# Moving the gate's row sums from the value projection into the attention stage, and giving the value copies five places instead of two

## The chip, the cores and the metric

The kernel runs on one core of a Trainium2 chip. The metric is the device time of one execution in microseconds (us): 2908.87 us is the median of three runs of the kernel before (2906.5 to 2911.03). The core's engines work side by side, each through its own fixed list of instructions in order: PE (matrix products), DVE (vector engine), ACT (activations and copies), POOL (GpSimd) and SP, which here only issues DMA transfers. They wait for one another through semaphores.

## The reference

Two attention blocks read the same x (2048 rows of 1024) and are mixed by a gate, all in float32:

```python
g = sigmoid((x * gate_w).sum(-1, keepdims=True))   # the gate: one number per row of x
a = linear_attention(x, A_wqkv, A_wo)   # 32 heads of 32; phi(t) = where(t>0, t+1, exp(t)) + 1e-6
b = softmax_attention(x, B_wqkv, B_wo)  # 32 heads of 32, 2048 x 2048 scores each
return g * a + (1 - g) * b
```

The gate needs, for each of the 16 blocks of 128 rows, a product of x with gate_w and a sum over its 1024 columns. It is used first where the queries of the linear attention are divided (g) and at the output (1 - g).

## The kernel before, in words

Every large matrix product is done as three products of "hi" and "lo" parts (lines 146 to 148 in `three`), so one product of a block of 128 rows with 512 columns is 8 x 3 = 24 matmuls, called a unit here.

The program has three parts. First (0 to 401 us) q, k and half of v of the softmax attention are computed; POOL and DVE prepare operands there (lines 253 and 409 to 414). Second (401 to 534 us), the stream `linear()` computes the second half of v in 16 "v" units; between their matmuls the stream `maxima()` puts score matmuls (line 902) whose row maxima DVE takes with a reduce (line 907). Third (from 534 us), the softmax heads run (`heads_()`: score matmuls of line 1053, exponentials on ACT in line 1057, products with v in line 1149), and at the same time maxima of a later head and the units of the linear attention: 64 units of keys and values ("kv"; a chunk is 16 units), 32 of queries, 32 of output. In this stage the sums of the exponentials are split: POOL adds 1536 of 2048 columns with one add per block (lines 1098 and 1102), DVE the other 512 (line 1111), which it keeps in a PSUM bank.

The order is written out by a planner at build time: it keeps a clock `T` per engine, takes the stream that is ready or furthest behind, and lets it issue. PSUM has a ring of six banks for all streams: a matmul can start in a bank only after the reader of that bank's former content has ended. Work on DVE that may come later is handed to `defer(fn, at, cost, rank)` and issued by `fill` where the planner's clock of DVE has room, or by `need` where something depends on it. An engine then goes through its list strictly in order.

The gate before (function `gate`, called by `next(gating, None)` at the end of each v unit): for each block t, two DMA loads of x into a quarter each of big[20] (line 334), and two DVE instructions SCALAR_TENSOR_TENSOR (line 344) that multiply by gate_w (in `zrep`) and sum along the row; both inputs lie in SBUF. One block is loaded ahead. After the sixteenth block follow an add, an Exp on ACT (line 347), and three small DVE instructions.

At the end of a v unit, ACT copies the unit's bank to a tile in SBUF (line 365), which SP sends to DRAM (line 366). The tile alternates between mid[10] and mid[11]. At the end of the last v unit the weights of the next chunk arrive by DMA (line 260), ACT and DVE split them (lines 571 and 573), and the copy of the unit's bank stands behind that on ACT.

Of the kernel before, what the change touches and what calls it, by code (L numbers as in the profile page):

```python
# [11 lines left out]
AF = mybir.ActivationFunctionType  # L12
ALU = mybir.AluOpType
# [5 lines left out]
P = 128  # L19
DH = 32  # L20
C = 512
# [24 lines left out]
def kernel(  # L46
# [107 lines left out]
    def use(eng, cost, *after):  # L154

        T[eng] = max(T[eng], *after, 0.0) + cost
        return T[eng] + LATENCY[eng]
# [142 lines left out]
    PAIRS = [(j, j + 1) for j in range(0, NJ, 2)]  # L300
    tmp = f32(big[20])
    s1, u2, u3 = [tmp[:, i * C:(i + 1) * C] for i in range(3)]
    gate_x = [tmp[:, i * C:(i + 1) * C] for i in range(4)]

    def xop(name, p, i):
        return big[XO[name][p]][:, i * C:(i + 1) * C]
# [20 lines left out]

    HD = D // 2
    nc.sync.dma_start(zrep, bass.AP(tensor=gate_w.tensor, offset=gate_w.offset, ap=[[0, P], [1, D]]))

    def gate():
        def load(t):
            for i in range(2):
                nc.sync.dma_start(gate_x[t % 2 * 2 + i], x[t * P:(t + 1) * P, i * HD:(i + 1) * HD])

        load(0)
        for t in range(NT):
            yield
            if t + 1 < NT:
                load(t + 1)  # L340
            for i in range(2):
                gx = gate_x[t % 2 * 2 + i]
                use("dve", 0.7)
                nc.vector.scalar_tensor_tensor(gx, gx, 1.0, zrep[:, i * HD:(i + 1) * HD], op0=ALU.mult,
                                               op1=ALU.mult, accum_out=tg[:, i, t:t + 1])
        nc.vector.tensor_add(tg[:, 0], tg[:, 0], tg[:, 1])
        nc.scalar.activation(tg[:, 0], tg[:, 0], AF.Exp, scale=-1.0)
        nc.vector.tensor_scalar_add(tg[:, 0], tg[:, 0], 1.0)
        nc.vector.reciprocal(g_sb, tg[:, 0])
        nc.vector.tensor_scalar(omg_sb, g_sb, -1.0, 1.0, op0=ALU.mult, op1=ALU.add)  # L350

    def spill(js):

# [10 lines left out]
    def v_out(c, t, ps, va):  # L364
        nc.scalar.copy(va, ps)
        nc.sync.dma_start(v_d[c][:, t, :], va)
# [75 lines left out]
        nc.sync.dma_start(qk_d[sec][0][g][:, sl], f32(hi))  # L442
        nc.sync.dma_start(qk_d[sec][1][g][:, sl], f32(lo))

    gating = gate()
    xp_done = set()

    def first_xp(n):
# [249 lines left out]
    def queries(n, c, t, pq, todo):  # L698
# [19 lines left out]
        give(b, 0.0, [item])  # L718
        o_left.append(item)

    def linear():
        extra = iter(())
        coming_w = deque()
        for n, (i, t) in enumerate(units):
            kind, c = chunks[i]
            pos = n % NT
            here_ = n < NT // 2
            follow = chunks[i + 1] if i + 1 < len(chunks) else None
            xp = xp_t[n % 2]
            yield bank_at  # L730
            b = take()
            ps = bank[b]
            T["pe"] = max(T["pe"], free[b])
            lin_kind[0] = kind
            if kind in ("q", "o") and c == 0 and t in (2, 8, NT - 2):
                yield lambda: None if mix_here else 0.0
                if t < NT - 2:
                    load_mix()
            if n < 2:
                load_head(n)  # L740
                load_v(n)
            for k in range(NK):
                yield lambda: ended(w_left[k], w_ready[k], 0.0 if here_ else xp_ready[n % 2])
                need(w_left[k])
                if here_:
                    jj, tt = divmod(n, TPC)
                    stat = [xop(PLACE[jj][k // HK], p, k % HK)[:, tt * P:(tt + 1) * P] for p in range(2)]
                else:
                    stat = [blocks(xp, p)[:, k] for p in range(2)]
                for m, _ in enumerate(three(ps, stat, (wpart(k, 0), wpart(k, 1)), k)):  # L750
                    lin_pe(1.0)
                    if m < 2:
                        yield always
                if k == 0 and n + 7 == len(units) and not o_main[0]:
                    load_o(0)
                if k == 1 and n + 1 == len(units):
                    split_o(0, slice(0, NK - 1))
                if k == NK // 2 and n + 1 == len(units) and over["head"]:
                    split_o(1, slice(0, NK - 1))
                if k == NK - 1:  # L760
                    yield from extra
                if follow and follow[0] == "o":
                    if pos == NT - 1:
                        w_left[k].clear()
                        yield lambda: 0.0 if mixed.count((k // HK, follow[1])) == 4 else None
                        load_wa(follow[1], k)
                    continue
                if follow and pos == NT - 2 and k < min(LEAD_W, NK):
                    coming_w.append(load_w(*follow, k, LEAD_W + 1))
                if follow and pos == NT - 1:  # L770
                    split_w(*follow, k, *coming_w.popleft(), nc.vector if kind == "v" else nc.gpsimd)
                    if k + LEAD_W < NK:
                        coming_w.append(load_w(*follow, k + LEAD_W, LEAD_W + 1))
            if NT // 2 <= n + 2 < len(units):
                load_xp(n + 2)
            for _ in range(1 + (n == 1) if n < NT else 0):
                next(gating, None)
            extra = iter(())
            e, r = mid[3 + n % 3], mid[6]
            if kind == "v":  # L780
                give(b, use("act", 0.5, T["pe"] + LATENCY["pe"]))
                v_out(c, t, ps, mid[10 + t % 2])
            elif kind == "kv":
                va = mid[7][:, (n % 2) * HC:(n % 2 + 1) * HC]
                yield from keys_alone(n - 2)
                nc.scalar.copy(va, ps[:, HC:])
                use("act", 0.28, T["pe"] + LATENCY["pe"])
                end = phi(ps, e, HC)

                def more(end, c=c, t=t, e=e, ps=ps):  # L790
                    pk = e[:, :HC]
                    nc.vector.scalar_tensor_tensor(pk, pk, 1.0, ps[:, :HC], op0=ALU.min, op1=ALU.add)
                    z_end[c % 2] = use("pool", 0.69, end)
                    if t == 0:
                        nc.gpsimd.tensor_copy(zsum[c % 2], pk)
                    else:
                        nc.gpsimd.tensor_add(zsum[c % 2], zsum[c % 2], pk)

                todo = [defer(more, end, 0.34)]
                give(b, 0.0, todo)  # L800
                keys(n, c, t, e, va, todo)
                if t == NT - 1:
                    extra = keysum(c)
            elif kind == "q":
                yield lambda: None if n - 3 not in turned and chunks[units[n - 3][0]][0] == "q" else 0.0
                end = phi(ps, e, C)
                d = dn[n % 2]

                def sums(_, e=e, ps=ps):
                    nc.vector.scalar_tensor_tensor(ps, e, 1.0, ps, op0=ALU.min, op1=ALU.add)  # L810

                def scaled(_, c=c, ps=ps, r=r):
                    nc.vector.tensor_mul(r, ps, zrep[:, c * C:(c + 1) * C])

                last = []

                def dens(end, r=r, d=d, last=last):
                    nc.vector.tensor_reduce(d, r.rearrange("p (h d) -> p h d", d=DH), AX.X, ALU.add)
                    nc.scalar.add(d, d, eps)
                    last[0].at = use("act", 0.2, end)  # L820

                def divide(_, t=t, e=e, ps=ps, d=d):
                    nc.vector.reciprocal(d, d)
                    nc.vector.scalar_tensor_tensor(
                        e.rearrange("p (h d) -> p h d", d=DH), ps.rearrange("p (h d) -> p h d", d=DH),
                        g_sb[:, t:t + 1], d.unsqueeze(2).to_broadcast([P, C // DH, DH]),
                        op0=ALU.mult, op1=ALU.mult)

                todo = chain(((sums, 0.63), (scaled, 0.63), (dens, 0.63), (divide, 0.9)), end)
                last.append(todo[-1])  # L830
                give(b, 0.0, todo)
                tasks.append((lambda todo=todo: both(ended(todo + o_left), bank_at()),
                              lambda n=n, c=c, t=t, e=e, todo=todo: queries(n, c, t, e, todo)))
            else:
                res = mid[(7, 10)[n % 2]]
                give(b, use("act", 0.5, T["pe"] + LATENCY["pe"]))
                nc.scalar.copy(res, ps)
                nc.sync.dma_start(ra_d[t][:, c * C:(c + 1) * C], res)
        over["lin"] = True
        load_all()  # L840
# [548 lines left out]
```

## Time and profile before

| | before |
|---|---|
| median of 3 runs | 2908.87 us |
| the profiled execution, its own time | 2906.63 us |
| span of that execution on the core | 2904.8 us |
| busy share: PE, DVE, ACT, POOL | 98%, 77%, 55%, 64% |
| mean DMA rate | 138 GB/s |

The span is the time from the first to the last instruction in the trace; the execution's own time is 1.8 us longer. A busy share is an average over the three parts, and says little of any one of them: POOL, for instance, is idle through the v units and almost always busy in the attention stage.

### The profile page before, as it was taken

To read this page: it belongs to the slowest core of one execution; us is meant where nothing else is said; L and a number is where in the kernel's file an instruction comes from. 1 tells how busy PE (TensorE), PEld (TensorE's weight loads), DVE (VectorE), ACT (ScalarE), POOL (GpSimd) and SP (SyncE) were. 2 spreads that over 40 slices of the span, in tenths; PEclk is the share of its full clock that TensorE was granted. 3 is DMA by queue.
4 is the path that set the end of the run, shared out by engine and by line. 5 is a ranking of instruction groups with operands and counts; after the bars stand their busy time and mean duration, and the time that the engine had idled before them with its cause. 6 is when DMAs were issued, how large, how long until landed. Compare 5 with 4: busy or idle time off the path is not lost.

```text
span 2904.8 us, 44336 instructions
## 1 busy us (share of the span) xinstructions
PE 2847.1 (98%) x15744; PEld 2039.5 (70%) x15744; DVE 2227.9 (77%) x3715; ACT 1596.8 (55%) x2976; POOL 1853.9 (64%) x646
## 2 busy tenths in 40 slices
PE   9999989899999999999999999799999999999999
PEld 7888867666666766666666666467676666766787
DVE  6667638788888888888888888688888887886522
ACT  5334320566676667666666666456666665666410
POOL 1212220488798889987988888468777878785000
PEclk9999999999999999999999999899999999999999
DMA  5957765423332324233323235444455344524542
GB/s 174 291 173 216 243 202 189 156 91 98 99 117 76 93 88 120 89 102 92 117 80 91 88 120 165 157 166 146 146 175 182 112 146 127 153 88 140 171 158 78
DMA packets 302496, 400.55 MB, mean 138 GB/s; under 512 B 92682, under 2 KB 185354, under 8 KB 299146
## 3 DMA queue, kind: packets, MB, share of 16 engines
q1 hardware_dynamic: 302276, 397.73, 44.3%
q8 instruction: 124, 2.03, 0.3%
q14 instruction: 96, 0.79, 0.1%
HBM read 287.57 MB, written 108.79 MB: 136 GB/s over the span
## 4 chain that ended last, share of the span: by engine, by line
PE 94%; DMA 3%; DVE 2%; ACT 0%; issue 0%; SPq 0%; ACTq 0%; DVEq 0%
PE bank L1053 16%; PE bank L902 16%; PE bank L1149 15%; PE bank L146 11%; PE bank L148 10%; PE bank L147 10%; PE bank L430 3%; PE bank L432 3%; PE bank L431 3%; PE bank L472 1%; PE bank L955 1%; PE bank L470 1%; PE bank L471 1%; DMA big<-xs 1%; DMA big<-qk 0%; PE bank L707 0%
## 5 line engine op out<-in xcount | busy, mean ns | idle before, releaser
L1102 POOL TENSOR_TENSOR big<-big,big 128x1536 f32<-128x1536 f32 (+1 forms) x434 | 1556.5, 3586 | 209.0 <-ACT big L1057 186.9
L907 DVE TENSOR_REDUCE mx<-bank 128x1 f32<-128x512 f32 x2048 | 1308.7, 680 | 306.7 <-PE bank L902 301.8
L1057 ACT ACTIVATE big<-bank 128x512 f32<-128x512 f32 x2048 | 1180.1, 601 | 528.1 <-PE bank L1053 457.8
L902 PE MATMUL bank<-big,big 128*128 128x512 f32 x2048 | 804.8, 393 | 21.6 <-DVE mx L907 11.9
L1053 PE MATMUL bank<-big,big 128*128 128x512 f32 x2048 | 810.7, 397 | 2.2 <-ACT big L1057 2.0
L146 PE MATMUL bank<-big,big 128*128 128x512 f32 x1408 | 554.6, 394 | 25.4 <-DMA big<-xs 21.4
L148 PE MATMUL bank<-big,big 128*128 128x512 f32 x1408 | 552.6, 392 | 1.0 <-DMA big<-oA 0.8
L147 PE MATMUL bank<-big,big 128*128 128x512 f32 x1408 | 552.8, 393 | 0.0
L1053 PEld LDWEIGHTS bank<-big,big 128*128 128x128 f32 x2048 | 384.4, 188 | 159.8 <-issue 62.8
L902 PEld LDWEIGHTS bank<-big,big 128*128 128x128 f32 x2048 | 385.9, 188 | 106.4 <-DVE mx L907 12.6
L1149 PE MATMUL bank<-big,mid 128*32 128x512 f32 x4096 | 459.2, 593 | 0.0
L146 PEld LDWEIGHTS bank<-big,big 128*128 128x128 f32 x1408 | 265.8, 189 | 91.2 <-issue 19.2
L1149 PEld LDWEIGHTS bank<-big,mid 128*32 128x32 f32 x4096 | 127.7, 110 | 263.6 <-issue 263.6
L148 PEld LDWEIGHTS bank<-big,big 128*128 128x128 f32 x1408 | 266.0, 189 | 58.5 <-DMA big<-oA 1.2
L147 PEld LDWEIGHTS bank<-big,big 128*128 128x128 f32 x1408 | 265.9, 189 | 55.4
L1111 DVE TENSOR_TENSOR bank<-bank,big 128x512 f32<-128x512 f32 (+1 forms) x434 | 280.2, 646 | 7.6 <-ACT big L1057 5.7
L1098 POOL TENSOR_TENSOR big<-big,big 128x1536 f32<-128x1536 f32 (+1 forms) x31 | 111.6, 3601 | 264.7 <-issue 141.1
L253 DVE TENSOR_TENSOR big<-mid,big 128x512 fp32r<-128x512 f32 x216 | 152.8, 731 | 83.9 <-ACT big L252 83.8
L409 POOL TENSOR_TENSOR mid<-mid,mid 128x512 f32<-128x512 f32 x16 | 20.7, 1291 | 278.3 <-DVE big L253 265.3
L252 ACT CAST big<-mid 128x512 fp32r<-128x512 f32 x216 | 130.2, 624 | 100.9 <-POOL mid L410 55.3
L431 PE MATMUL bank<-big,big 128*128 128x512 f32 x448 | 174.3, 389 | 0.0
L432 PE MATMUL bank<-big,big 128*128 128x512 f32 x448 | 174.3, 389 | 0.0
(102 smaller groups left out, 1949.8 us busy)
## 6 DMA issues: line engine op xcount, KB each, us to landing
big<-xs SPq DMA_DIRECT2D x208, 512.0 KB
qk<-mid SPq DMA_DIRECT2D x128, 256.0 KB
big<-oA SPq DMA_DIRECT2D x64, 512.0 KB
big<-qk SPq DMA_DIRECT2D x96, 256.0 KB
big<-qk SPq DMA_DIRECT2D x384, 64.0 KB
mid<-in_b_wqkv SPq DMA_DIRECT2D x88, 256.0 KB
xs<-big SPq DMA_DIRECT2D x64, 256.0 KB
oA<-mid SPq DMA_DIRECT2D x64, 256.0 KB
```

The source lines that it names most:

```text
L146: yield nc.tensor.matmul(ps, sh, mh_, start=(kt == 0), stop=False)
L147: yield nc.tensor.matmul(ps, sh, ml_, start=False, stop=False)
L148: yield nc.tensor.matmul(ps, sl, mh_, start=False, stop=(kt == NK - 1))
L431: nc.tensor.matmul(ps, sh, ml_, start=False, stop=False)
L432: nc.tensor.matmul(ps, sl, mh_, start=False, stop=(i == HK - 1))
L902: nc.tensor.matmul(bank[b], q[:, t * P:(t + 1) * P], k[:, j * C:(j + 1) * C], start=True, stop=True)
L907: nc.vector.tensor_reduce(m[:, t, j:j + 1], bank[b], AX.X, ALU.max)
L1053: nc.tensor.matmul(bank[b], k[:, t * P:(t + 1) * P], q[:, j * C:(j + 1) * C], start=True, stop=True)
L1057: nc.scalar.activation(pr_t[i][:, j * C:(j + 1) * C], bank[b], AF.Exp, scale=SCALE)
L1102: nc.gpsimd.tensor_add(lacc[:, :qp], lacc[:, :qp], pr(t)[:, :qp])
L1111: nc.vector.tensor_add(lacc[:, qp:] if t == NT - 1 else l_b[:, :n], l_b[:, :n], src)
L1149: nc.tensor.matmul(av_b[j * DH:(j + 1) * DH, :], v[:, t, :], pr(t)[:, j * C:(j + 1) * C], start=(t == 0), stop=(t == NT - 1))
```

## The change: what it does

The generator `gate()` with its early start is gone. A function `gate(t)` is called at the end of the last v unit and of the first sixteen kv units (units 15 to 31). It first issues what is left of the previous block's work (`need`), then loads the two halves of block t into mid[8] and mid[9], and defers the two SCALAR_TENSOR_TENSOR instructions (planned at 8 us after the planner's PE clock, 0.7 us each, rank 2). The last call does the final arithmetic. So the same 32 loads and 32 instructions are issued, in kv units instead of v units. The copies of v's second half go round mid[10], mid[11], mid[7], mid[8], mid[9].

```diff
-    gate_x = [tmp[:, i * C:(i + 1) * C] for i in range(4)]
...
-    def gate():
-        def load(t):
-            for i in range(2):
-                nc.sync.dma_start(gate_x[t % 2 * 2 + i], x[t * P:(t + 1) * P, i * HD:(i + 1) * HD])
-
-        load(0)
-        for t in range(NT):
-            yield
-            if t + 1 < NT:
-                load(t + 1)
-            for i in range(2):
-                gx = gate_x[t % 2 * 2 + i]
-                use("dve", 0.7)
-                nc.vector.scalar_tensor_tensor(gx, gx, 1.0, zrep[:, i * HD:(i + 1) * HD], op0=ALU.mult,
-                                               op1=ALU.mult, accum_out=tg[:, i, t:t + 1])
-        nc.vector.tensor_add(tg[:, 0], tg[:, 0], tg[:, 1])
...
-    gating = gate()
...
+    def gate(t):
+
+        need(gates)
+        gates.clear()
+        at = T["pe"] + 8.0
+        for i in range(2 if t < NT else 0):
+            gx = mid[8 + i]
+            nc.sync.dma_start(gx, x[t * P:(t + 1) * P, i * HD:(i + 1) * HD])
+
+            def part(_, i=i, gx=gx):
+                nc.vector.scalar_tensor_tensor(gx, gx, 1.0, zrep[:, i * HD:(i + 1) * HD], op0=ALU.mult,
+                                               op1=ALU.mult, accum_out=tg[:, i, t:t + 1])
+
+            gates.append(defer(part, at, 0.7, 2))
+        if t == NT:
+            nc.vector.tensor_add(tg[:, 0], tg[:, 0], tg[:, 1])
...
+            use("dve", 0.8)
...
-            for _ in range(1 + (n == 1) if n < NT else 0):
-                next(gating, None)
+            if NT - 1 <= n < 2 * NT:
+                gate(n - NT + 1)
...
-                v_out(c, t, ps, mid[10 + t % 2])
+                v_out(c, t, ps, mid[(10, 11, 7, 8, 9)[n % 5]])
```

On DVE, at the third v unit, where the first maxima stand. Names: `mx` is the tile of maxima, `bank5` a PSUM bank, `big20` the loaded x, `zrep` gate_w, `tg` the gate's sums. Before:

```order
L253 TENSOR_TENSOR big19_227<-mid13_242,big19_227 128x512
L344 SCALAR_TENSOR_TENSOR big20_228,tg_199<-big20_228,zrep_196 128x512 x6
L907 TENSOR_REDUCE mx0_200<-bank5_248 128x1
L907 TENSOR_REDUCE mx0_200<-bank6_249 128x1
L907 TENSOR_REDUCE mx0_200<-bank0_243 128x1
```

After:

```order
L253 TENSOR_TENSOR big19_227<-mid13_242,big19_227 128x512
L908 TENSOR_REDUCE mx0_200<-bank5_248 128x1
L908 TENSOR_REDUCE mx0_200<-bank6_249 128x1
L908 TENSOR_REDUCE mx0_200<-bank0_243 128x1
L908 TENSOR_REDUCE mx0_200<-bank1_244 128x1
```

Six gate instructions stood ahead of the first maximum; now none does, and none stands among the other maxima of the v units.

On DVE, in the attention stage, where a head's sums are inverted (RECIPROCAL) and its result is scaled. Names: `kvb` is the sum of the linear attention's keys times values, `mid11` the head's result, `big9`/`big10` exponentials, `bank7` DVE's part of their sum, `mid8` and `mid9` the loaded x. Before:

```order
L1111 TENSOR_TENSOR bank7_250<-bank7_250,big9_3822 128x512
L907 TENSOR_REDUCE mx0_200<-bank0_243 128x1
L617 TENSOR_TENSOR kvb_195<-bank3_246,kvb_195 128x64
L962 RECIPROCAL bank2_245<-bank2_245 128x128 x4
L965 TENSOR_TENSOR mid11_240<-mid11_240,bank2_245 128x512
L907 TENSOR_REDUCE mx0_200<-bank1_244 128x1
```

After:

```order
L1112 TENSOR_TENSOR bank7_250<-bank7_250,big9_3755 128x512
L908 TENSOR_REDUCE mx0_200<-bank2_245 128x1
L908 TENSOR_REDUCE mx0_200<-bank1_244 128x1
L594 TENSOR_TENSOR kvb_195<-bank0_243,kvb_195 128x64
L708 SCALAR_TENSOR_TENSOR mid8_237,tg_199<-mid8_237,zrep_196 128x512
L708 SCALAR_TENSOR_TENSOR mid9_238,tg_199<-mid9_238,zrep_196 128x512
L963 RECIPROCAL bank6_249<-bank6_249 128x128 x4
L966 TENSOR_TENSOR mid11_240<-mid11_240,bank6_249 128x512
L908 TENSOR_REDUCE mx0_200<-bank1_244 128x1
```

One pair of gate instructions now stands ahead of the reciprocals and of the maxima behind them. There are 16 such pairs in the kv units; ten stand together like this one, the other six have maxima between the two.

On SP, in the v units. Names: `v1` is the second half of v in DRAM, `in_x` the input x, `mid13<-v0` the load of a head's v. Before:

```order
L886 DMA mid13_242<-v0_160 128x16x32
L334 DMA big20_228<-in_x 128x512 x4
L366 DMA v1_161<-mid11_240 128x512
L334 DMA big20_228<-in_x 128x512 x2
L366 DMA v1_161<-mid10_239 128x512
```

After:

```order
L887 DMA mid13_242<-v0_160 128x16x32
L344 DMA v1_161<-mid11_240 128x512
L344 DMA v1_161<-mid7_236 128x512
L344 DMA v1_161<-mid8_237 128x512
L344 DMA v1_161<-mid9_238 128x512
```

The loads of x have left this stretch, and three more tiles take the copies of v. PE's list is the same before and after up to the first kv unit; from there to the end of the sixteenth a few matmuls change places, and behind it the lists agree again.

## Rows read from the trace of the kernel before

**Rows 1.** The page's busy time: busy us, share of the span, instructions.
```profile
PE 2847.1 (98%) x15744; PEld 2039.5 (70%) x15744; DVE 2227.9 (77%) x3715; ACT 1596.8 (55%) x2976; POOL 1853.9 (64%) x646
```

**Rows 2.** Waits of PE, whole span: us in total, times, longest us.
```profile
PE bank L146 <- DMA big<-xs: 21.4, 2, 15.0
PE bank L902 <- DVE mx L907: 11.9, 1, 11.9
PE bank L902 <- ACT mid L365: 9.5, 2, 6.8
```

**Rows 3.** Timeline of PE, third v unit: start, us, instruction [idle before <-releaser].
```profile
421.53 0.39 PE L146 MATMUL bank<-big,big 128*128 128x512 f32 x1
424.56 0.79 PE L902 MATMUL bank<-big,big 128*128 128x512 f32 x1 [2.64 <-ACT mid L365]
...
438.49 0.80 PE L902 MATMUL bank<-big,big 128*128 128x512 f32 x1 [11.86 <-DVE mx L907]
439.08 0.63 PE L147 MATMUL bank<-big,big 128*128 128x512 f32 x1
...
441.58 0.39 PE L146 MATMUL bank<-big,big 128*128 128x512 f32 x1
441.81 0.39 PE L147 MATMUL bank<-big,big 128*128 128x512 f32 x1
```

**Rows 4.** Timeline of ACT, same stretch.
```profile
423.92 0.58 ACT L365 COPY mid<-bank 128x512 f32<-128x512 f32 x1 [11.35 <-DMA v<-mid]
```

**Rows 5.** Timeline of DVE, same stretch.
```profile
434.85 0.69 DVE L344 SCALAR_TENSOR_TENSOR big<-big,zrep 128x512 f32<-128x512 f32 x1 [11.07 <-DMA big<-in_x]
...
437.75 4.40 DVE L907 TENSOR_REDUCE mx<-bank 128x1 f32<-128x512 f32 x7
```

**Rows 6.** Timeline of PE, from the last v unit into the first kv unit.
```profile
522.45 0.39 PE L148 MATMUL bank<-big,big 128*128 128x512 f32 x1
...
526.90 0.40 PE L147 MATMUL bank<-big,big 128*128 128x512 f32 x1
534.15 0.79 PE L902 MATMUL bank<-big,big 128*128 128x512 f32 x1 [6.85 <-ACT mid L365]
...
537.21 0.39 PE L146 MATMUL bank<-big,big 128*128 128x512 f32 x1
```

**Rows 7.** Timeline of ACT, same stretch.
```profile
529.16 2.06 ACT L571 CAST big<-mid 128x512 fp32r<-128x512 f32 x3 [4.93 <-DMA mid<-in_a_wqkv]
533.41 0.22 ACT L347 ACTIVATE tg<-tg 128x16 f32<-128x16 f32 x1 [2.19 <-DVE tg L346]
533.53 0.57 ACT L365 COPY mid<-bank 128x512 f32<-128x512 f32 x1
```

**Rows 8.** Windows: stretch, its length, busy us of each engine, granted clock, DMA share, GB/s.
```profile
510.00:530.00 20.00, 15.17 (x66) 11.92 (x64) 10.75 (x21) 5.01 (x9) 0.00 (x0) 1.00 0.90 303
540.00:850.00 310.00, 310.00 (x1899) 212.01 (x1898) 265.19 (x455) 206.23 (x400) 269.21 (x96) 1.00 0.31 95
```

**Rows 9.** Waits of DVE from 540 to 850 us.
```profile
DVE mx L907 <- PE bank L902: 41.2, 14, 4.5
```

**Rows 10.** POOL's groups from 540 to 850 us: count, busy us, mean ns, idle before.
```profile
L1102 POOL TENSOR_TENSOR big<-big,big 128x1536 f32<-128x1536 f32 x67 | 234.6, 3502 | 20.7 <-ACT big L1057 17.5
```

**Rows 11.** Timeline of DVE in the first part, beside POOL's adds.
```profile
256.80 0.68 DVE L493 TENSOR_TENSOR big<-bank,big 128x512 f32<-128x512 f32 x1
257.40 1.40 DVE L253 TENSOR_TENSOR big<-mid,big 128x512 fp32r<-128x512 f32 x1
260.63 1.11 DVE L253 TENSOR_TENSOR big<-mid,big 128x512 fp32r<-128x512 f32 x1 [1.83 <-ACT big L252]
```

**Rows 12.** Timeline of POOL, same stretch.
```profile
256.96 1.28 POOL L409 TENSOR_TENSOR mid<-mid,mid 128x512 f32<-128x512 f32 x1 [4.65 <-DVE big L253]
258.32 1.62 POOL L410 TENSOR_TENSOR mid<-mid,mid 128x512 f32<-128x512 f32 x1
259.90 1.29 POOL L411 TENSOR_TENSOR mid<-mid,mid 128x512 f32<-128x512 f32 x1
```

More of the change, by code (lines that the diff above doesn't have):

```diff
@@ L329 @@
     nc.sync.dma_start(zrep, bass.AP(tensor=gate_w.tensor, offset=gate_w.offset, ap=[[0, P], [1, D]]))
-    def gate():
-        def load(t):
-            for i in range(2):
-                nc.sync.dma_start(gate_x[t % 2 * 2 + i], x[t * P:(t + 1) * P, i * HD:(i + 1) * HD])
-        load(0)
-        for t in range(NT):
-            yield
-            if t + 1 < NT:
-                load(t + 1)
-            for i in range(2):
-                gx = gate_x[t % 2 * 2 + i]
-                use("dve", 0.7)
-                nc.vector.scalar_tensor_tensor(gx, gx, 1.0, zrep[:, i * HD:(i + 1) * HD], op0=ALU.mult,
-                                               op1=ALU.mult, accum_out=tg[:, i, t:t + 1])
-        nc.vector.tensor_add(tg[:, 0], tg[:, 0], tg[:, 1])
[L347 to L350, printed above, removed]
     def spill(js):
@@ L719, in queries @@
         o_left.append(item)
+    def gate(t):
[11 more added lines that the diff above has]
+            nc.vector.tensor_add(tg[:, 0], tg[:, 0], tg[:, 1])
+            nc.scalar.activation(tg[:, 0], tg[:, 0], AF.Exp, scale=-1.0)
+            nc.vector.tensor_scalar_add(tg[:, 0], tg[:, 0], 1.0)
+            nc.vector.reciprocal(g_sb, tg[:, 0])
+            nc.vector.tensor_scalar(omg_sb, g_sb, -1.0, 1.0, op0=ALU.mult, op1=ALU.add)
+            use("dve", 0.8)
+    gates = []
     def linear():
```

## The prediction, made before the changed kernel ran

> **What bounds the kernel now.** I read the busy times first: PE is busy 2847 us of the span, 98% [rows 1]. So the change can only win where PE stands idle or runs slowly, and can only lose by making new idle time. The waits of PE come next, since they name those places: 21.4 us for a transfer late in the kernel, which the change does not touch, 11.9 us of a line-902 matmul for a DVE maximum, and 9.5 us for a copy of line 365 on ACT [rows 2]. The timelines then show where the last two lie: around 422 to 441 us, in the v units [rows 3], and at 527 to 534 us, where the v units end [rows 6]. In the attention stage from 540 to 850 us, where the gate's work goes, PE has no idle time at all, DVE is busy 265 of 310 us and POOL 269 [rows 8]. That stage is bound by PE, with DVE close behind.
>
> **What goes: the stall in the third v unit.** PE stops twice here [rows 3]. The first stop ends with the ACT copy of line 365, which waited 11.35 us for the transfer out of its tile [rows 4]: the tile had been used two units earlier, and that transfer stood in SP's queue behind the loads for the heads. With five tiles this copy goes to a fresh one. The second stop, 11.86 us, is on a maximum that DVE had not taken, because ahead of it in DVE's list stood gate sums that waited for x until 434.85; the seven maxima run at once from 437.75 [rows 5]. With the gate gone, DVE can take them as they come. From 421.53 to 441.58 twelve matmuls start. At the 0.23 us apart that the last two rows of the stretch show they would need 2.7 us; they took 20.05. The excess, 17.3 us, holds both stops and the slow matmuls behind them, which end at 0.63 us instead of 0.39 [rows 3]. What is late next? PE's list here is unchanged and the head's loads served the matmuls at 417 to 421 us without a wait, so I see nothing late and take all 17.3. At the worst (the maxima wait for k instead) nothing of it is won.
>
> **What goes: the end of the v units.** From 522.45 to 537.21 seventeen matmuls start, which need 3.9 us; the excess is 10.9 [rows 6]. PE waits for the copy at 533.53. On ACT that copy stands behind the split of the last weights, which waited for their transfer until 529.16 and ends at 531.22, and then behind the gate's Exp, which waited for DVE until 533.41 [rows 7]. Without the Exp the copy starts 2.3 us sooner. The weights also come sooner: two blocks of x, four transfers of 0.26 MB, no longer stand among them, and at 303 GB/s [rows 8] 1.05 MB is 3.5 us. So PE goes on 5.8 us sooner, and of the 1.5 us lost on slow matmuls behind the stop (seven in 3.06 us) I take 1.1 back, since the stop becomes short. Together 6.9 us; the ends are 2.3 (the Exp alone) and 10.9 (the whole excess). The new loads of the first block at the end of this unit stand behind the weights in SP's list and ahead of nothing that is needed soon.
>
> **What is added: 32 gate instructions on DVE in the kv units.** By their own 0.69 us [rows 5] they are 22 us. DVE has 310 - 265 = 45 us of idle time there [rows 8], 41.2 of it in 14 waits of up to 4.5 us [rows 9], while PE multiplies by v and gives DVE no new maximum; the planner puts most pairs into those. So 22 us are hidden and 23 us of cover are left.
>
> But these instructions have two inputs in SBUF, and POOL is not idle here as it is in the v units. A row of the first part shows what that does: a DVE instruction of line 253 with two SBUF inputs starts at 257.40, takes 1.40 us instead of 0.69, and ends 0.56 us after the end of POOL's add of 256.96; the next, at 260.63, ends 0.55 us after the end of the add of 259.90 [rows 11, 12]. POOL's add of 258.32, which came behind the first, took 1.62 us instead of 1.29. The instruction of 256.80, with one input in PSUM, is not slowed by the same add. Twenty rows of line 253 are lengthened like this. So I read: a gate sum waits for the end of the POOL add that runs, and holds the next one up by about 0.3 us. In the attention stage an add takes 3.5 us [rows 10] and POOL is busy 87% of the time [rows 8].
>
> The Trainium skill says the same on its page "SBUF — State Buffer", section "Who interferes with whom": DVE's second input comes through a read port that it shares with GpSimd, and whoever starts first keeps it for the whole instruction. The rows agree for adds of 1.3 us. For adds of 3.5 us no row shows it: if the hold had the length seen in the rows (at most 1.3 us) the waits would be about 32 x 0.6 = 19 us and hidden, while by the page they grow with the add.
>
> I price it with the long hold. A sum that comes at any moment waits 0.87 x 1.75 = 1.5 us. The second of a pair meets the add that came in between: 3.5 us if POOL has one ready, nothing if POOL has run out of exponentials, which it does in most of the same stretches (POOL's idle 41 us); I take 1.5 again. That makes 48 us, less the 23 of cover: 25 us. DVE's maxima are then late, and PE with them, as its next score matmuls need the banks. I take a third off, by choice, because PE has other streams' matmuls and up to six banks ahead of it: 17 us. The ends are 0 (covered) and 32 x 3.5 - 23 = 89 us. POOL's own delay, 32 x 0.3 = 10 us, fits its idle 41 us. The final Exp now stands on ACT among the exponentials and waits for DVE: 1 us, between 0 and the 2.2 us that it waited in the v units [rows 7]. The 32 loads of x cost nothing here: 8.4 MB on engines that are busy 31% [rows 8]. If one came late, DVE would stand still in front of it.
>
> **The sum.** -17.3 - 6.9 + 17 + 1 = -6.2 us. Against the profiled execution's 2906.6 us that is 2900.4; the median of the runs is 2.2 us higher, so 2902.7.
>
> **The rivals.** *Covered:* the waits fit DVE's idle time. For it: the planner puts many pairs just where POOL runs dry. Against it: the pair ahead of four reciprocals, and the six pairs with maxima between them, stand where DVE has no idle time. Then -24.2: 2884.7. *POOL decides:* the first sum of a pair waits half an add, the second a whole one, so 16 x 5.25 = 84 us, less 23 is 61, less a third 41, and the sum is -24.2 + 41 + 1 = +18: 2926.7, slower. It speaks for this that an add is nearly always waiting behind the running one, against it POOL's idle 41 us. The point: 24.2 us are lost again when the 32 waits reach 23 + 35 = 58 us, 1.8 us each. *The stall stays:* the maxima of the third v unit find another thing late, such as k. Then -6.9 + 18 = +11: 2920. Against it: DVE's seven maxima run without a pause once the gate sums are done [rows 5], so their matmuls were there. That the change does not do what it says I exclude by the order of DVE's and SP's lists.
>
> **How the numbers follow.** My sum, with its loss between 5 and 30 us (2890 to 2916): 0.52; covered 0.23; POOL decides 0.17; the stall stays 0.08. What a measurement of this kernel can tell from no change is about 0.2%, 5.8 us. My sum lies just at that edge: of its 0.52 I give 0.24 to faster, 0.20 to the same and 0.08 to slower. Covered is faster (0.23). POOL decides gives 0.02 to the same and 0.15 to slower; the stall stays 0.02 and 0.06. Together faster 0.47, same 0.24, slower 0.29. The range goes from the covered case, 2883, to where POOL decides, 2927; the likeliest case alone is 2890 to 2916.
>
> **What would show it.** In the trace of the changed kernel: PE without a stop from 400 us to the end of the v units, about 17 us sooner; the copy of line 344 (365 before) right behind the last weight split, with a stop of PE of some 2 us there; the gate's instructions (line 708) in kv units at 0.7 to 5 us, mean near 2.2, each long one ending 0.55 us after an add of POOL; and in that stage waits of PE for DVE maxima, some 17 us in sum, where there were none. The prediction is wrong if line 708 stays at 0.7 us, if PE still stops at 422 us, or if the kv units' length grows by more than 30 us.

## The result and the profile after

The changed kernel takes 2922.37 us (median of 5 runs, 2916.43 to 2924.32) against 2908.50 for the kernel before (2906.50 to 2911.03, 5 runs on the same chip). The ratio is 1.0044, with a 95% interval of 1.0030 to 1.0059: slower by 13.9 us. The prediction was 2902.7 us, faster by 6; the time lies inside its range, on the other side of no change. The profiled execution of the kernel after took 2924.32 us, its span is 2922.5.

In the kernel after, most line numbers have moved; the names below give both.

| | before | after |
|---|---|---|
| gate sum | L344 | L708 |
| last add, Exp, and the three that make the gate | L346, L347 to L350 | L713, L714 to L717 |
| copy of v on ACT | L365 | L343 |
| maximum on DVE; matmul into its bank | L907; L902, L1053 | L908; L903, L1054 |
| POOL's long add, exponential on ACT | L1102, L1057 | L1103, L1058 |

PE is busy for 2863.4 us, 16.3 us more than before with the same 15744 matmuls, and DVE 2281.6 instead of 2227.9 [rows 1]. The page's busy times of after:

```profile
PE 2863.4 (98%) x15744; PEld 2044.2 (70%) x15744; DVE 2281.6 (78%) x3715; ACT 1598.8 (55%) x2976; POOL 1858.4 (64%) x646
```

More busy time with equal work means matmuls that run slowly, and DVE instructions that last longer.

**The v units are as predicted.** In the third unit PE goes on without a stop, where it had stopped twice [rows 3]. PE's timeline of after:

```profile
421.25 0.39 PE L903 MATMUL bank<-big,big 128*128 128x512 f32 x1
...
422.38 0.39 PE L903 MATMUL bank<-big,big 128*128 128x512 f32 x1
...
511.70 0.80 PE L903 MATMUL bank<-big,big 128*128 128x512 f32 x1 [3.07 <-ACT mid L343]
512.29 0.63 PE L148 MATMUL bank<-big,big 128*128 128x512 f32 x1
```

On ACT the copy of the fourth unit, and that of the last with the split of the weights ahead of it [rows 7]; the copy of the third now ran at 418.05 instead of 423.92 [rows 4]:

```profile
425.07 0.59 ACT L343 COPY mid<-bank 128x512 f32<-128x512 f32 x1 [6.44 <-PE bank L148]
...
509.12 2.04 ACT L548 CAST big<-mid 128x512 fp32r<-128x512 f32 x3 [4.39 <-DMA mid<-in_a_wqkv]
511.07 0.58 ACT L343 COPY mid<-bank 128x512 f32<-128x512 f32 x1
```

The copy of the fourth unit comes 16.7 us sooner than before (441.82), that of the last one, at 511.07, 22.5 us sooner than at 533.53. The first part of the kernel ran 0.6 us later in this execution, so the gains are 17.35 and 5.7 us, 23.1 in all. The stop of 3.07 us and 13 slow matmuls behind it are left.

**The kv units give it back and more.** I set the k-th exponential on ACT of one trace beside that of the other. The 17th is 23.2 us ahead of before, the 33rd (at 551 us) 12.9, the 257th (785 us) 1.2; the 305th, at 853 us, is 15.4 us behind, and from 910 to 1960 us that stays between 14.3 and 14.9. So some 38 us are lost in 525 to 853 us. The k-th matmul of PE tells the same: 22.4 us ahead at the end of the v units, 14.3 behind at the end of the kv stretch, 36.7 in all. That is more than the 30 us that the prediction named as a sign of being wrong. In the same stretch the waits of PE, none before between 540 and 850 us [rows 8], add up to 21.4 us. The view of PE's waits from 520 to 900 us, after (its last line, 1.5 us in two waits for maxima, is left out):

```profile
PE bank L1054 <- DVE mx L908: 9.6, 6, 4.3
PE bank L1054 <- DVE mid L966: 5.4, 2, 2.7
PE bank L1054 <- ACT big L1058: 4.9, 1, 4.9
```

About 7 us more are 33 matmuls that start 0.43 us apart instead of 0.23, most of them right after such stops. The rest, some 9 us, I could not assign; it is not idle time, since all gaps of PE in this stretch, the shortest included, come to 21.5 us.

**Where the time of a gate sum goes.** The view of line 708 (count, then shortest, median and longest in ns):

```profile
L708 DVE SCALAR_TENSOR_TENSOR mid<-mid,zrep x32: 669/2305/3949, 526.9 to 831.5; 128x512 f32<-128x512 f32 x32
```

The 32 sums take 68.4 us where 22 would do: 46.3 us of waiting. The timelines of DVE and, in the second fence, of POOL at the first two pairs:

```profile
526.92 3.27 DVE L708 SCALAR_TENSOR_TENSOR mid<-mid,zrep 128x512 f32<-128x512 f32 x1
...
530.12 3.95 DVE L708 SCALAR_TENSOR_TENSOR mid<-mid,zrep 128x512 f32<-128x512 f32 x1
...
537.53 3.63 DVE L708 SCALAR_TENSOR_TENSOR mid<-mid,zrep 128x512 f32<-128x512 f32 x1
...
541.09 0.68 DVE L708 SCALAR_TENSOR_TENSOR mid<-mid,zrep 128x512 f32<-128x512 f32 x1
...
541.71 2.47 DVE L908 TENSOR_REDUCE mx<-bank 128x1 f32<-128x512 f32 x4
```

```profile
522.55 10.97 POOL L1103 TENSOR_TENSOR big<-big,big 128x1536 f32<-128x1536 f32 x3
...
537.17 3.44 POOL L1103 TENSOR_TENSOR big<-big,big 128x1536 f32<-128x1536 f32 x1 [1.10 <-ACT big L1058]
```

The sum of 537.53 ends at 541.16, 0.55 us after the end of the add of 537.17 (540.61); all 20 sums that take more than 1 us end so. The second sum of that pair meets no add, since POOL waits for an exponential, and takes 0.68. Four maxima stood behind the pair, and PE waited for one of them (its timeline, after):

```profile
542.44 0.80 PE L1054 MATMUL bank<-big,big 128*128 128x512 f32 x1 [4.29 <-DVE mx L908]
543.03 0.63 PE L146 MATMUL bank<-big,big 128*128 128x512 f32 x1
```

**The end of the sums is worse than any pair.** DVE's timeline where the last sum and the gate's final arithmetic stand, and then ACT's:

```profile
831.49 3.35 DVE L708 SCALAR_TENSOR_TENSOR mid<-mid,zrep 128x512 f32<-128x512 f32 x1
...
834.88 1.11 DVE L713 TENSOR_TENSOR tg<-tg 128x16 f32<-128x16 f32 x1
836.27 0.94 DVE L715 TENSOR_SCALAR tg<-tg 128x16 f32<-128x16 f32 x1 [0.28 <-ACT tg L714]
837.24 0.25 DVE L716 RECIPROCAL g_sb<-tg 128x16 f32<-128x16 f32 x1
837.53 3.09 DVE L717 TENSOR_SCALAR omg_sb<-g_sb 128x16 f32<-128x16 f32 x1
840.54 1.27 DVE L908 TENSOR_REDUCE mx<-bank 128x1 f32<-128x512 f32 x2
```

```profile
836.02 0.22 ACT L714 ACTIVATE tg<-tg 128x16 f32<-128x16 f32 x1 [5.11 <-DVE tg L713]
...
837.46 1.08 ACT L1058 ACTIVATE big<-bank 128x512 f32<-128x512 f32 x2
```

ACT stands still for 5.11 us in front of the Exp, with exponentials queued behind it, because the last sum waits for POOL and the add of L713 stands behind that sum. PE then lacks banks (its timeline, after; the windows below it show busy time of PE, PEld, DVE, ACT and POOL, granted clock, DMA share and GB/s):

```profile
838.11 0.80 PE L1054 MATMUL bank<-big,big 128*128 128x512 f32 x1 [4.89 <-ACT big L1058]
838.70 0.63 PE L146 MATMUL bank<-big,big 128*128 128x512 f32 x1
```

```profile
838.00:842.00 4.00, 3.23 (x7) 1.99 (x7) 4.00 (x4) 1.14 (x3) 4.00 (x3) 0.50 0.00 0
...
520.00:835.00 315.00, 297.31 (x1765) 199.26 (x1763) 308.02 (x479) 188.98 (x361) 253.51 (x88) 0.98 0.37 114
```

Behind the stop the granted clock is 0.50, the lower of the two levels (1.2 GHz), and a matmul takes 0.63 us instead of 0.39. Between 826 and 853 us 10 us go. The last row is the whole stretch: DVE counts as busy in 308 of 315 us. It has become the engine that PE waits for most (16.5 of the 21.4 us).

### The profile page after: what moved, and what is told of

Read it like the earlier page. It is cut to its first block, busy times and chain, and to the rows that moved or that the text cites. A ratio compares the mean times of both kernels' runs of the same rounds, so it can differ in the third digit from the quotient of the medians.

```text
span 2922.5 us, 44334 instructions
## 1 busy us (share of the span) xinstructions
PE 2863.4 (98%) x15744; PEld 2044.2 (70%) x15744; DVE 2281.6 (78%) x3715; ACT 1598.8 (55%) x2976; POOL 1858.4 (64%) x646
## 4 chain that ended last, share of the span: by engine, by line
PE 90%; DVE 6%; DMA 2%; issue 1%; ACT 0%; SPq 0%; ACTq 0%; DVEq 0%
PE bank L1054 15%; PE bank L903 15%; PE bank L1150 14%; PE bank L146 10%; PE bank L148 10%; PE bank L147 10%; PE bank L410 3%; PE bank L408 3%; PE bank L409 3%; DVE mx L908 3%; DVE mid L708 1%; PE bank L447 1%; PE bank L449 1%; PE bank L448 1%; PE bank L956 1%; DMA big<-xs 1%
## 5 line engine op out<-in xcount | busy, mean ns | idle before, releaser
L1103 POOL TENSOR_TENSOR big<-big,big 128x1536 f32<-128x1536 f32 (+1 forms) x434 | 1559.7, 3594 | 235.0 <-ACT big L1058 211.0
L908 DVE TENSOR_REDUCE mx<-bank 128x1 f32<-128x512 f32 x2048 | 1312.1, 682 | 302.9 <-PE bank L903 299.1
L1058 ACT ACTIVATE big<-bank 128x512 f32<-128x512 f32 x2048 | 1181.3, 601 | 560.3 <-PE bank L1054 493.2
L1054 PE MATMUL bank<-big,big 128*128 128x512 f32 x2048 | 816.4, 400 | 21.2 <-DVE mx L908 9.6
L903 PE MATMUL bank<-big,big 128*128 128x512 f32 x2048 | 808.3, 395 | 4.9 <-ACT mid L343 3.1
L146 PE MATMUL bank<-big,big 128*128 128x512 f32 x1408 | 555.9, 395 | 23.7 <-DMA big<-xs 21.4
L1054 PEld LDWEIGHTS bank<-big,big 128*128 128x128 f32 x2048 | 387.0, 189 | 183.9 <-issue 58.7
L903 PEld LDWEIGHTS bank<-big,big 128*128 128x128 f32 x2048 | 387.6, 189 | 93.4 <-DVE mx L908 4.5
```

The source lines that it names most:

```text
L146: yield nc.tensor.matmul(ps, sh, mh_, start=(kt == 0), stop=False)
L903: nc.tensor.matmul(bank[b], q[:, t * P:(t + 1) * P], k[:, j * C:(j + 1) * C], start=True, stop=True)
L908: nc.vector.tensor_reduce(m[:, t, j:j + 1], bank[b], AX.X, ALU.max)
L1054: nc.tensor.matmul(bank[b], k[:, t * P:(t + 1) * P], q[:, j * C:(j + 1) * C], start=True, stop=True)
L1058: nc.scalar.activation(pr_t[i][:, j * C:(j + 1) * C], bank[b], AF.Exp, scale=SCALE)
L1103: nc.gpsimd.tensor_add(lacc[:, :qp], lacc[:, :qp], pr(t)[:, :qp])
```

## The experiments

My theory for the first five: the v units' gain is real; the sums lose it by waiting for POOL, because both their inputs are in SBUF; and the Exp costs far more than the 1 us foreseen. The rivals: the sums cost by standing ahead of maxima whatever POOL does, and the final arithmetic costs little by itself. Each kernel was timed in five rounds beside the kernel before (median 2908.88 us for the first four, 2910.05 for the last three).

**The sums with one input in PSUM.**

```diff
-                nc.vector.scalar_tensor_tensor(gx, gx, 1.0, zrep[:, i * HD:(i + 1) * HD], op0=ALU.mult,
+                nc.vector.scalar_tensor_tensor(gx, gx, 1.0, l_b, op0=ALU.mult,
```

> The changed kernel, with one input of the 32 gate sums taken from a PSUM bank (DVE's own running sum) instead of gate_w in SBUF; the gate's value is thereby another one, and nothing else is changed. Theory P (a DVE instruction with two SBUF inputs waits for the POOL add that runs, and the lateness passes to PE): the sums take 0.69 us each instead of 2.14 on average, PE's stops on DVE between 520 and 805 us go, the final arithmetic's cost stays; 22 us of lateness are gone, so 2900 us (2893 to 2906). Rival L (the 22 us of work as such, or its place in DVE's list, makes DVE late): the sums may be short, but the time stays within 5 us of the changed kernel's 2922.

Measured: 2893.48 us, ratio 0.9948 (0.9936 to 0.9961). The view of line 708, and PE's waits from 400 to 900 us:

```profile
L708 DVE SCALAR_TENSOR_TENSOR mid<-mid,bank x32: 665/675/686, 524.3 to 804.7; 128x512 f32<-128x512 f32 x32
```

```profile
PE bank L1054 <- ACT big L1058: 4.4, 1, 4.4
PE bank L903 <- ACT mid L343: 3.0, 1, 3.0
PE bank L1054 <- DVE mx L908: 0.4, 1, 0.4
```

The lists of PE, DVE, ACT and POOL are the same as in the kernel after, instruction for instruction, but for this one input; no sum waits, and 28.9 us come back (2922.37 - 2893.48). So not the sums' place in DVE's list but their wait for POOL costs the time. The stop of the final arithmetic is still there (4.4 us).

**The five places alone**, put into the kernel before.

```diff
-                v_out(c, t, ps, mid[10 + t % 2])
+                v_out(c, t, ps, mid[(10, 11, 7, 8, 9)[n % 5]])
```

> The kernel before with only the five places for the copies of v. Theory P: the first stop of PE in the third v unit (2.6 us) goes, but the maxima still stand behind gate sums that wait for x until about 435 us, so the second stop takes over what the first gives: 2908 us (2904 to 2910). Rival (the places alone free the third v unit): 17 us less, 2891.

Measured: 2907.03 us, ratio 0.9999 (0.9990 to 1.0008). PE's waits from 400 to 900 us (two lines, 2.4 us for the next weights, are left out):

```profile
PE bank L902 <- DVE mx L907: 15.0, 1, 15.0
PE bank L902 <- ACT mid L365: 6.7, 1, 6.7
```

Before, the third unit had a stop of 2.64 us for the copy and one of 11.86 for the maximum [rows 3]; now it is one of 15.0 for the maximum. The x of the gate comes as late as it did, and the places alone win nothing.

**The gate moved alone**, with two places as before.

```diff
-                v_out(c, t, ps, mid[(10, 11, 7, 8, 9)[n % 5]])
+                v_out(c, t, ps, mid[10 + t % 2])
```

> The changed kernel with the copies of v in two places as before. Theory P: with the gate gone from the v units, PE now reaches the fourth unit's copy while the second unit's transfer still stands behind the head loads on SP, so the copies stop PE by 3 to 8 us that the five places had removed: 2927 us (2924 to 2931). Rival (the places are worth nothing): within 2 us of the changed kernel, 2922.

Measured: 2924.24 us, ratio 1.0053 (1.0040 to 1.0065), which overlaps with that of the kernel after. The copy on ACT still waits for its tile, and PE for the copy (a fence for each):

```profile
429.31 0.58 ACT L343 COPY mid<-bank 128x512 f32<-128x512 f32 x1 [9.73 <-DMA v<-mid]
```

```profile
429.95 0.50 PE L903 MATMUL bank<-big,big 128*128 128x512 f32 x1 [2.24 <-ACT mid L343]
```

The trace shows what five places are worth once the gate is gone: a stop of 2.24 us and little behind it. By the end of the v units PE has gained 20.8 us on the kernel before instead of 23.0. The times (1.9 us apart) fit that but can't tell it from nothing. I had expected a larger difference; its size stays undecided.

**The final arithmetic early**, at the end of the last v unit.

```diff
+    nc.vector.memset(tg, 0.0)
...
+        if t == 0:
+            nc.vector.tensor_add(tg[:, 0], tg[:, 0], tg[:, 1])
+            nc.scalar.activation(tg[:, 0], tg[:, 0], AF.Exp, scale=-1.0)
...
-        if t == NT:
-            nc.vector.tensor_add(tg[:, 0], tg[:, 0], tg[:, 1])
-            nc.scalar.activation(tg[:, 0], tg[:, 0], AF.Exp, scale=-1.0)
...
```

> The changed kernel with the gate's final arithmetic (add, Exp on ACT, three small DVE instructions) moved to the end of the last v unit, where POOL is idle; it works on zeros there, so the gate is one half everywhere. Theory P (the final arithmetic costs about 10 us where it stands, because ACT waits for it and its small SBUF instructions wait for POOL): 2912 us (2908 to 2916), and no stop of PE of 4.9 us on the exponentials near 833 us. Rival (that stop comes from the late sums in front of it, not from the final arithmetic): 2921 or more.

Measured: 2909.50 us, ratio 1.0002 (0.9993 to 1.0011): 12.9 us less than the kernel after. PE's waits from 400 to 900 us:

```profile
PE bank L1055 <- DVE mid L967: 5.3, 2, 2.6
PE bank L1055 <- DVE mx L909: 4.9, 5, 2.4
PE bank L904 <- DVE mx L909: 4.9, 3, 2.4
PE bank L904 <- ACT mid L344: 4.0, 1, 4.0
```

The stop for an exponential (L1058) is gone, and stops for DVE stay. But the 12.9 us are not the price of five small instructions alone. The `use` call moved with them, so the planner placed the first pairs otherwise: up to 863 us, 118 places of PE's list hold another matmul than in the kernel after, and five maxima now stand between the first two sums. The stop of 4.29 us that PE had at 542 us, some 290 us ahead of the place that the final arithmetic left, is nearly gone too. PE's only wait between 535 and 560 us here:

```profile
538.70 0.50 PE L1055 MATMUL bank<-big,big 128*128 128x512 f32 x1 [0.33 <-DVE mx L909]
```

So the time lies where I expected it, in part by another cause than the one named, and this run shows that the final arithmetic costs something, not how much. The table behind the run with both edits comes closer.

**POOL without most of its adds** in the heads.

```diff
-            nc.gpsimd.tensor_add(lacc[:, :qp], lacc[:, :qp], pr(t)[:, :qp])
```

> The changed kernel without POOL's adds for the third to last block of each head (the sums of the exponentials lack these blocks); the planner's clocks and every other instruction stay. The gate sums keep two inputs in SBUF. Theory P (they wait for POOL's adds): all sums take 0.69 us, the final arithmetic is short too, PE's stops on DVE go: 2889 us (2882 to 2896). Rival R (two SBUF inputs are slow here for another reason, or DVE is late for its own load): the sums keep a mean above 1.5 us and the time stays above 2910.

Measured: 2887.09 us, ratio 0.9922 (0.9908 to 0.9935). The view of line 708:

```profile
L708 DVE SCALAR_TENSOR_TENSOR mid<-mid,zrep x32: 662/685/1161, 526.5 to 806.2; 128x512 f32<-128x512 f32 x32
```

Both inputs are in SBUF as in the kernel after, and the median is 685 ns. With the first experiment this closes the chain: the wait needs the second SBUF input and POOL's long add; without either it is gone.

**The PSUM input and the early final arithmetic together.**

> The first and the fourth experiment together: one input of the gate sums from PSUM, and the final arithmetic at the end of the last v unit (on zeros). Theory P: nothing of the change's cost is left and only its gain of 23.4 us stays, 2885 us (2882 to 2888). Rival (part of the loss has a third cause, such as the loads of x or the new order of the kv units): above 2890.

Measured: 2886.81 us, ratio 0.9920 (0.9907 to 0.9934). Its window of the kv stretch and PE's only wait from 400 to 900 us:

```profile
520.00:835.00 315.00, 314.99 (x1952) 214.33 (x1954) 285.52 (x523) 208.60 (x402) 273.20 (x97) 1.00 0.40 119
```

```profile
PE bank L904 <- ACT mid L344: 4.2, 1, 4.2
```

With the sums on DVE, but none waiting, PE is full again: 1952 matmuls in 315 us against 1765 after. The 32 sums and the 32 loads of x by themselves are hidden but for 2 to 3 us (the table below).

I set PE's k-th matmul in the trace of each kernel beside the one of the kernel before, at four places of PE's list (us later than before, a minus for sooner; where two lists differ by an exchange, a value may be off by about 1 us):

| at, in the kernel before | after | sums from PSUM | final arithmetic early | both |
|---|---|---|---|---|
| 534 us, the end of the v units | -22.4 | -23.9 | -21.8 | -21.0 |
| 580 us | -12.3 | -23.6 | -19.0 | -19.9 |
| 820 us, ahead of the final arithmetic | 4.5 | -22.3 | 1.5 | -19.1 |
| 880 us | 14.3 | -15.4 | 6.6 | -18.5 |

Between 820 and 880 us the final arithmetic makes the difference: 6.9 us are lost against 0.6 with both edits where no sum waits (6.3 us), and 9.8 against 5.1 where the sums wait (4.7 us). Between 534 and 580 us the kernel after loses 10.1 us and the one with the final arithmetic early only 2.8; there the order of the first pairs is another one. By 820 us 3.0 of that are left. At 880 us the two traces are 7.7 us apart; what the medians differ beyond that (12.9) is not found in this stretch.

These runs make an account of the change, by medians: gain 23.2 us (2910.05 - 2886.81); waits of the sums 28.9 (2922.37 - 2893.48, two kernels with the same lists); final arithmetic 6.7 (2893.48 - 2886.81; these two lists of PE differ in 65 places, but the table puts the loss where the final arithmetic stands). Net +12.4 against the measured +13.9; the medians of the kernel before in the two series differ by the missing 1.5, so each term is good to 1 or 2 us. Taken in the other order the terms would be 22.7 (2909.50 - 2886.81) and 12.9, but that way leads over the kernel whose order the planner changed. Only their sum, 35.6, is free of that choice.

**A version of the whole computation** follows from it: the gate's sums go back into the v units, where POOL is idle, but as deferred work. They are spread over units 4 to 12, their x is loaded six blocks ahead into eight half-tiles and one tile more, and the final arithmetic stands in unit 14. The five places stay.

```diff
+    gate_x = [tmp[:, i * C:(i + 1) * C] for i in range(4)] + [mid[i] for i in (3, 4, 5, 6)]
...
-    def gate(t):
+    def gate(n):
...
+        if n == 3:
+            spare = big_tile(15, F32)
+            gate_x.extend(spare[:, i * C:(i + 1) * C] for i in range(4))
+        for _ in range({4: 3, 5: 2, 6: 2, 7: 2, 8: 2, 9: 2, 10: 1, 11: 1, 12: 1}.get(n, 0)):
+            t = len(gates)
+            need(gates[t - 6] if t > 5 else [])
...
+                items.append(defer(part, T["pe"] + 8.0, 0.7, 2))
...
+        if n == 14:
...
-            if NT - 1 <= n < 2 * NT:
-                gate(n - NT + 1)
+            gate(n)
```

> A version that keeps the whole computation: five places for the copies, and the gate back in the v units, where POOL is idle, but from the fifth unit on (units 4 to 12, up to six blocks loaded ahead into tiles that are free there), its sums deferred work on DVE, the final arithmetic at the end of the fifteenth. Theory P: the gain of both stretches stays (no sums ahead of the first maxima, no loads of x among the next chunk's weights, no Exp ahead of the last copy), and nothing is paid in the attention stage: 2886 us (2882 to 2891). Rival (DVE or DMA has no room for the gate in these units): stops of PE there, 2895 to 2908.

Measured: 2886.34 us, ratio 0.9920 (0.9906 to 0.9933), 36 us below the kernel after. The view of its sums (line 713 here) and of PE's waits from 400 to 900 us:

```profile
L713 DVE SCALAR_TENSOR_TENSOR big<-big,zrep x20: 681/684/697, 439.8 to 482.5; 128x512 f32<-128x512 f32 x20
L713 DVE SCALAR_TENSOR_TENSOR mid<-mid,zrep x12: 671/683/694, 445.3 to 496.7; 128x512 f32<-128x512 f32 x12
```

```profile
PE bank L146 <- DMA big<-xs: 3.2, 1, 3.2
PE bank L910 <- ACT mid L344: 2.2, 1, 2.2
```

No sum waits, and the stops of 14.5 us in the third unit [rows 3] do not come back, though the gate is in the v units, if only from the fifth on: what stalled PE was the late x in front of the first maxima [rows 5], not the amount of the gate's work.

## Why the prediction was wrong, point by point

**The gains were right.** The third unit: 17.35 us for 17.3. The end of the v units: 5.7 for 6.9, with a stop of 3.07 us where "some 2" were foreseen. The experiments put both together at 23.2.

**The hold by a long add was right.** Rows of 1.3 us adds [rows 11, 12] were stretched to adds of 3.5 us, and the sums wait 46.3 us for the 48 worked out, with the predicted 0.55 us behind the add's end. That a DVE instruction with two SBUF inputs is blocked by a POOL instruction that reads SBUF and started first is what the Trainium skill states on its page "SBUF — State Buffer", section "Who interferes with whom"; the trace agrees, with waits up to 3.26 us on one sum (3.95 - 0.69).

**The step that failed first: "I take a third off, by choice, because PE has other streams' matmuls and up to six banks ahead of it."** No row carried that. The waits less DVE's idle time made 25 us; the run with one input in PSUM shows 28.9, not the 17 taken. PE had been busy in all of the 310 us [rows 8], so there was no moment at which it could make up for a stop: what went beyond DVE's idle time went to PE whole. The slow matmuls behind the new stops came on top; the prediction had counted such matmuls among its gains, and put none into its loss.

**The second: the final Exp, "1 us, between 0 and the 2.2 us that it waited in the v units".** It measured about 6.7 us. I took the price from a place where POOL is idle and DVE short of work. In the kv units the Exp waits for a DVE add that stands behind the last sum, and it holds up ACT's exponentials, for which PE waits in turn. I also priced the four small DVE instructions of L713 to L717 at nothing; L717 alone took 3.09 us beside POOL's add, with two maxima behind it.

With 17 put to 28.9 and 1 to 6.7 the predicted sum, -6.2, becomes +11.4; measured were +13.9.

**The rivals.** *Covered* (2884.7) falls: the sums cost 28.9 us. *The stall stays* (2920) falls by PE's timeline at 421 us, though its time was near. *POOL decides* (2926.7) came within 4.3 us, on the right side, but by luck and not by its mechanism: it needed 84 us of waits; measured were 46.3, or 1.45 a sum, and half of the second sums met no add. By the prediction's own point the change should have lost only from 58 us of waits on. That it lost with 46.3 is due to the third that was taken off and to the final arithmetic.

**Open.** After 1960 us the profiled execution of after first gains 1 us and then falls back by some 4 (between 2350 and 2400 us), far from anything that the change touches. The traces of the other kernels move there by up to 5 us either way as well, the five places alone by 2, so I take it for the single execution, without having shown that. And what the five places add to the moved gate is between nothing and a few us.

## What to carry to other kernels

Before work is moved to an engine with idle time, ask who else reads SBUF there: a two-input instruction costs its own time plus a good part of the other engine's running instruction, and it belongs where that engine is idle, or with one input in PSUM. When the waits exceed that idle time and the engine that bounds the kernel has none of its own, count the excess in full. A tiny result that crosses to another engine is priced by what stands ahead of its producer and behind its consumer, not by its 0.2 us.

## What the runs showed of the hardware that was not expected

- A DVE instruction with a single small SBUF input can wait as long as one with two: TENSOR_SCALAR of 128x16 (L717) took 3.09 us and ended at 840.62, just behind POOL's add, while RECIPROCAL of the same shape (L716) took 0.25 us during that same add. POOL's timeline there, after, and the same instruction in the run without most of POOL's adds, where it took 0.17 us (174 ns):

```profile
837.14 3.46 POOL L1103 TENSOR_TENSOR big<-big,big 128x1536 f32<-128x1536 f32 x1
```

```profile
L717 DVE TENSOR_SCALAR omg_sb<-g_sb x1: 174/174/174, 808.4 to 808.4; 128x16 f32<-128x16 f32 x1
```

  The Trainium skill's page "SBUF — State Buffer" states, in the section "Who interferes with whom", that TENSOR_SCALAR can enter a mode that takes the shared ports; the 3.09 us fit that. No run here tells whether it was in that mode.
- POOL loses too: an add that starts while a sum is still running takes 3.78 to 3.98 us instead of 3.5 [rows 10]; one that runs already when a sum comes keeps its 3.5.
- A stop of PE is paid again behind it: after the stops of 3.07 us (at 511 us) and 4.29 us (at 542 us), 12 to 13 matmuls took 0.63 us instead of 0.39, at a granted clock of 0.50.
- DVE's busy time contains the waits inside its instructions: 308.0 us after against 285.5 with the sums from PSUM and the final arithmetic early, although the latter got 523 instructions done in the window and the former 479. An engine that looks full may be waiting.
